# A two-dimensional FFT and a SwiGLU block on one core: rising rows of x in larger blocks, and a build-time planner that knows of DMA transfers

## The chip, the core and the metric

The kernel runs on one core of one Trainium2 chip. The core has five engines, each with its own instruction stream: TensorE (PE) multiplies matrices into PSUM, VectorE (DVE), ScalarE (ACT) and GpSimd (POOL) work elementwise, and SyncE (SP) here only issues DMA transfers. Sixteen DMA engines move the data. The metric is the device time of one execution in microseconds (us).

## The reference

```python
X = np.fft.fft(x, axis=1)          # x: (8, 3008, 256), float32
X = np.fft.fft(X, axis=2)
x = X.real.reshape(8 * 3008, 256)
g = x @ w_gate                     # (256, 1536)
silu = g * (1.0 / (1.0 + np.exp(-g)))
val = x @ w_val                    # (256, 1536)
out = silu * val @ w_out           # (1536, 256) -> (24064, 256)
```

So: the real part of a Fourier transform over sequence and feature, then a gated feed-forward block over 24064 rows.

## The kernel before, in words

**Tables instead of an FFT.** The transforms are matrix products with cosine and sine tables. The symmetries of the input are used first: rows of x and their mirror rows are folded into sums and differences, on the sequence axis (a rising and a falling set of rows) and on the feature axis. The transform over the feature axis is folded into the weights: Wp holds the weights times the cosines, Wq those times the sines, Wm and Wg are signed or scaled copies of Wq. After that each pair of output rows k and M-k comes from the same two vectors P and Q: the row is P W + Q W', its mirror P W - Q W'.

**Loading x.** For each batch b two groups of rows are loaded. XA takes 128 partitions, XC 60 (two batches side by side, one in the upper and one in the lower half). Each partition has eight pieces of 2 KB: four rising (`X3[.., 0:4, :]`), one from each quarter of the sequence, and four falling (`X3[:, 4 + a, :]`), the mirror rows. Rising rows want ascending addresses over the partitions, falling rows descending ones. The kernel therefore cuts the partitions into blocks of L (LA for XA, LC for XC; NA and NC_ are their numbers). The blocks stand in reverse order; within a block, rising rows ascend and falling rows descend. `load_a` (L179) issues NA rising transfers, one a block (L181), and four falling ones over all partitions (L183), whose pattern on the side of x is "NA blocks, then LA rows going down" (`down_set`, L173). `load_c` (L185) does the same for XC: L190 rising, L192 falling, L194 one extra row. In the kernel before LA, NA = 8, 16 and LC, NC_ = 4, 15 (L164, L165).

Batch 0 is loaded at the start by hand (L291 to L314): one rising transfer over all 128 partitions for XA (L291) and two of 64 for XC (L297), and falling rows in the same `down_set` pattern (`fall_a`, L294; `fall_c`, L301), some from SP's queue and some from ACT's. Its rising rows are put into the block order by a matrix product with the permutations putA and putC (`place`, L469); DVE then adds and subtracts (L478 for XA, L572 for XC), and the first transform follows.

**Folding and transforming later batches.** GpSimd folds each load in twelve steps (`fold_steps`, L200; the first of each half is L207, which waits for the load). SP moves the folded XC into a stack of two halves (St, L1285). PE multiplies by the tables (L1299), ACT copies one half (od, L1310) and DVE adds and subtracts into P and Q (L1324).

**The main loop.** The columns are cut into 24 tiles of 328 to 512, and each tile has 12 units (128 of the 1536 hidden columns each). A unit makes gate and value products (PE, L1003), takes them through SiLU (ACT, L1084 and L1115), and multiplies them (DVE L1107 and L1131, or POOL L1103 after an ACT copy, L1100; POOL L1144 for the mirrored half) into hp and hm. KINDS (L32) says for each unit of each tile how the row 0 terms get in and which engine does which part: three groups of twelve letters for gate, value and product. Where KINDS asks for it, the first row of Q, copied to all partitions, is added on DVE (L1069) or seeded into PSUM by ACT (L1059). That copy, bc, is made by two DMA transfers, Q to br (L1444) and br to bc (L1452), for each tile. When a tile is done, its output products (PE, L1171) are evicted by ACT (L1177, L1180) into one of eleven work slots (wk0s to wk10s) and stored by SP in pieces (L1183). The slots also hold the intermediate values of units.

**The planner.** From L806 on the order of all this is set at build time. Each piece is an Op with an engine, a duration, a delay until its result may be used (`lat`), its inputs and outputs. `Sched.run` goes through time, picks for each engine the earliest ready piece within a window, hands out slots and banks, and at the end issues everything in that order. SHIFT holds due times by kind of piece, WINDOW how far ahead an engine may reach. DMA transfers are pieces on SP; the planner also keeps eight `lanes`, since no more than eight transfers may be outstanding: the next one waits until the one eight before it has ended. `run_loads` (L1230) adds up to LOADS load transfers in each unit, and all that are left when the fold begins.

Of the kernel before, what the change touches and what calls it, by code (L numbers as in the profile page):

```python
# [36 lines left out]
    "000000020000 121121122112 DDPDDDDDDDDD",  # L37
    "020202000200 222111121112 DDDDDDPDDDDD",
    "000202020020 121112111211 DDPDDDDDDDDD",
    "002000002222 121211211211 DDDDPDDDDPDD",  # L40
    "020200000000 111211212122 DDDPDDDDDDDD",
    "002020020020 121211112111 PDDDDDDDDDDD",
    "020200000220 111222111112 DDPPDDDDDDDP",
    "002022000220 111122111111 DDPDPDDDDDDD",
    "000002002020 211212121211 PPDDDDDPDDDD",
    "020200000022 111211221112 DDPDDDDDDDPD",
    "020000000222 111112112121 PDDDDDPDDPDP",
    "000200000000 112211222111 DDPPDDDDPDDD",
    "200200202000 121111221211 DPPDPDDDPDDD",
    "220000200020 121211111111 DPDDDDPDDDDD",  # L50
    "002200200022 122111111111 DPDDPDDPPDDD",
    "202002020000 122111111111 DDPPPPPDDPDD",
    "020002220000 211211111111 DPDDDPDPDDDD",
    "002202000200 112211211121 DDDDPDPDDDDD",
    "220220000020 111111111121 PDDPDDPPPDPD",
    "020002220022 111112112211 DPDDPPDPDPDD",
]
# [7 lines left out]
def kernel(  # L65
# [8 lines left out]
    nc = tc.nc  # L74
    B, M, D = x.shape
    Dff = moe_w_gate.shape[1]
    P = 128
# [21 lines left out]
    NCR = GH - P  # L99
# [63 lines left out]

    LA, NA = 8, P // 8  # L164
    LC, NC_ = 4, NCR // 4  # L165

# [619 lines left out]
    for i in range(NS_FIRST, NS):  # L786
# [3 lines left out]
    LOAD_AT = 2  # L790
    LANE = 3.0
    LOAD_LAT = 10.0
    LOADS = 4
    GRP = 4
    WM_ACT = ((1, 0), (1, 1))
    SHIFT = dict(eg=-31.963, egc=-0.628, es=8.915, esc=0.39, ev=-0.141, fold=10.859, gm=5.523, hm=-1.136, hp=6.081,
                 hq=-3.52, od=-3.013, oth=4.215, out=-2.764, pe=-5.12, put=0.935, seedg=1.589, seedv=2.165,
                 sm=2.381, sp=0.129, val=-3.706, vm=5.929)
    WINDOW = {"DMA": 4.725, "PE": 13.96, "ACT": 10.324, "DVE": 14.0, "POOL": 14.0, "SP": 4.726}
    SEM = {"PE": 0.052, "ACT": 0.036, "DVE": 0.036, "POOL": 0.10, "SP": 0.06, "DMA": 0.0}  # L800
    TAIL = {"PE": 0.163, "ACT": 0.118, "DVE": 0.08, "POOL": 0.02, "SP": 0.0, "DMA": 0.0}
    BEGIN = {"DVE": 1.2, "ACT": 0.7, "POOL": 14.0, "PE": 0.0}
    FIFO = {"h": 2, "bc": 2, "br": 1, "pq": 5, "cp": 2, "fc": 1, "st": 3}
    ANY = {"B": 8, "S": NS, "Q": NQ}

    class Op:  # L806
        __slots__ = ("eng", "dur", "lat", "fn", "cat", "clock", "at", "n", "deps", "owners", "new", "start", "free", "end")

    class Sched:
# [11 lines left out]

        def add(self, eng, dur, fn, r=(), w=(), new=(), lat=None, cat="oth", bits=None, after=()):
            o = Op()
            o.eng, o.dur, o.fn, o.n = eng, dur, fn, len(self.ops)
# [24 lines left out]
            o.owners.update(o.new)  # L849
            self.ops.append(o)  # L850

        def run(self, begin, early):
# [25 lines left out]
            order = []  # L878
            lanes = [0.0] * 8

# [43 lines left out]
            while left:  # L924
# [26 lines left out]
                s, o = best  # L951
# [197 lines left out]
    class OWork:  # L1149
# [88 lines left out]
    def fold_step(what, i, unit):  # L1238
# [5 lines left out]
        def fn():  # L1244
            if j == 0:
# [11 lines left out]
        tmp = ("fold",)  # L1257
        r = {0: [((kind,), k) for k in range(40)], 1: [(tmp, "F")], 2: [(tmp, "F")], 3: [(tmp, "E"), (tmp, "O")],
             4: [(tmp, "A")], 5: [(tmp, "E"), (tmp, "O")]}[j]
# [21 lines left out]
    def spread_op(b):  # L1281
        for half, b_ in ((0, b), (1, b + 1)) if b > 1 else ((1, b),):
            for kind in range(2):
                def fn(half=half, b_=b_, kind=kind):
                    nc.sync.dma_start(out=stack(b_)[64 * kind:64 * kind + 64, :],  # L1285
                                      in_=foldC[b][64 * half:64 * half + 64, kind])
                S.add("SP", 0.6, fn, r=[(("fc", b), (q, k)) for q in range(2) for k in range(2)],
                      w=[(("st", b_), kind)], new=[("st", b_)], lat=3.0)

# [169 lines left out]
    S.hold("st", 0)  # L1459
    for fc, at in ((1, 0.0), (2, 6.0)):  # L1460
        for gv in range(2):
            S.add("DMA", 0.01, lambda: None, w=[(("W",), (fc, gv))], lat=at)
    S.add("DMA", 0.01, lambda: None, w=[(("pq", 0), "Q")], lat=0.8)
    S.add("DMA", 0.01, lambda: None, w=[(("Wo",), 0)], lat=9.0)
    prev = None
    owork = None
    U = [Unit(u) for u in units]
    for i, u in enumerate(units):
# [18 lines left out]
        for j, k in enumerate((i - ROW_GAP, i)[::-1]):  # L1487
            tr, fr = divmod(k, nF)
            if k >= 0 and fr == {0: 11, 1: 3, 2: 99}.get(tr, 6) and tr + 1 < nT:
                if j:  # L1490
                    S.add("SP", 0.55, all_rows(tr + 1), r=[(("br", tr + 1), 0)], w=[(("bc", tr + 1), 0)], new=[("bc", tr + 1)], lat=3.0)
                else:
                    S.add("SP", 0.55, first_rows16(tr + 1), r=[(("pq", tr + 1), "Q")], w=[(("br", tr + 1), 0)], new=[("br", tr + 1)], lat=2.6)
        if i == FIRST + 1:
# [59 lines left out]
```

## Time and profile before

| What | Value |
| --- | --- |
| Median of 3 runs | 634.14 us (631.53 to 634.88) |
| The profiled execution | 631.46 us |
| Its span, first to last instruction | 629.7 us |
| Mean granted TensorE clock | 0.995 |
| HBM read and written | 29.43 MB and 24.65 MB |

The profile was taken on the profiled execution alone. A busy row gives an engine's busy time and its share of the span. A row of waits says who waited, what ended the wait, the total, the count and the longest. A row of windows gives a stretch, then for each engine shown its busy time and instructions, then the granted clock, the mean busy share of the 16 DMA engines and GB/s. A chain is the work that ended last, followed back in time. Rows with "SPq" or "ACTq" are the issuing of transfers, not the transfers.

### The profile page before, as it was taken

The page shows a single profiled execution, that of the slowest core. Times are in us where ns is not written, and L with a number is a line of the kernel's source. Part 1 is how long each engine was busy: PE and PEld are TensorE (multiplying, and loading weights), DVE is VectorE, ACT ScalarE, POOL GpSimd, SP SyncE. Part 2 cuts the span into 40 slices and gives each one's busy share as a digit, 9 for nine tenths or more (in the row PEclk, how much of TensorE's full clock was granted, in tenths as well). Part 3 has the DMA queues.
Part 4 walks back from the last instruction along what each step waited for, and adds up shares of the span by engine and source line. Part 5 has one row for each costly group of instructions (what it writes and reads, how often), then busy time and mean ns, then how long its engine had stood idle before and what let it go on. Part 6 is the DMA issues. An engine that isn't in the chain of part 4 may idle for free.

```text
span 629.7 us, 12646 instructions
## 1 busy us (share of the span) xinstructions
PE 607.7 (97%) x4069; PEld 395.8 (63%) x4069; DVE 559.1 (89%) x1030; ACT 572.3 (91%) x1111; POOL 537.1 (85%) x495
## 2 busy tenths in 40 slices
PE   8999998999999899999999999998999999999997
PEld 6545664666556566666666666665666666666686
DVE  8989996988979799899998999877899999999982
ACT  7686667999989799999999999997999999999994
POOL 8878997999789889999999899998899867756782
PEclk9999998999999899999999999999999999999999
DMA  9954447242632712446136112227111112112112
GB/s 227 138 111 119 118 106 165 90 137 74 138 92 59 158 50 88 131 118 151 53 81 155 52 47 59 83 60 165 47 44 52 54 43 61 59 35 61 55 53 77
DMA packets 50736, 57.71 MB, mean 92 GB/s; under 512 B 7256, under 2 KB 37724, under 8 KB 50670
## 3 DMA queue, kind: packets, MB, share of 16 engines
q1 hardware_dynamic: 47016, 53.78, 32.8%
q0 software_dynamic: 3216, 2.36, 2.8%
q10 hardware_dynamic: 438, 0.77, 0.5%
q8 instruction: 32, 0.52, 0.4%
q14 instruction: 34, 0.28, 0.1%
HBM read 29.43 MB, written 24.65 MB: 86 GB/s over the span
## 4 chain that ended last, share of the span: by engine, by line
PE 62%; DMA 16%; POOL 8%; ACT 5%; issue 3%; SPq 3%; DVE 2%; ACTq 0%; POOLq 0%; DVEq 0%
PE ps L1003 31%; PE ps L1171 27%; DMA XA<-in_x_dram 7%; POOL hm L1144 3%; PE ps L1299 3%; DMA XA<-in_moe_w_val_dram 2%; DMA out_dram<-wk5s 1%; POOL SDf L207 1%; DMA br<-Qt 1%; DMA XC<-in_x_dram 1%; ACT ps L1059 1%; SPq L1183 1%; DMA out_dram<-wk1s 1%; DMA out_dram<-wk8s 1%; SPq L181 1%
## 5 line engine op out<-in xcount | busy, mean ns | idle before, releaser
L1003 PE MATMUL ps<-Pt,Wp 128*128 128x512 bf16 (+2 forms) x576 | 206.1, 376 | 8.5 <-ACT wk1s L1310 2.8
L1171 PE MATMUL ps<-Wo,hp 128*128 128x256 bf16 (+2 forms) x1140 | 167.5, 273 | 0.1
L1171 PE MATMUL ps<-Wo,hm 128*128 128x256 bf16 (+2 forms) x1140 | 166.5, 272 | 0.4 <-ACT wk0s L1177 0.3
L1003 PE MATMUL ps<-Qt,Wq 128*128 128x512 bf16 (+2 forms) x422 | 155.2, 377 | 1.9 <-DVE wk1s L1069 1.2
L1171 PEld LDWEIGHTS <-hm 128*128 128x128 bf16 (+2 forms) x1140 | 111.9, 98 | 63.4 <-issue 5.4
L1171 PEld LDWEIGHTS <-hp 128*128 128x128 bf16 (+2 forms) x1140 | 112.0, 98 | 62.7 <-issue 5.9
L1144 POOL TENSOR_TENSOR hm<-sv1q 128x1024 bf16<-128x1024 f32 (+2 forms) x68 | 126.6, 1862 | 25.5 <-ACT sv1q L1115 22.9
L1144 POOL TENSOR_TENSOR hm<-sv0q 128x1024 bf16<-128x1024 f32 (+2 forms) x68 | 126.6, 1862 | 20.8 <-ACT sv0q L1115 17.4
L1059 ACT ACTIVATE ps<-bc,w 128x512 f32<-128x512 bf16 (+2 forms) x154 | 112.4, 738 | 1.2 <-DVE hp L1107 0.3
L1003 PE MATMUL ps<-Qt,Wm 128*128 128x512 bf16 (+2 forms) x294 | 105.2, 376 | 2.6 <-ACT wk5s L1084 2.5
L1003 PEld LDWEIGHTS <-Wp 128*128 128x128 bf16 x576 | 56.5, 98 | 34.5 <-issue 7.1
L1115 ACT ACTIVATE sv0q<-ps 128x512 f32<-128x512 f32 (+2 forms) x101 | 68.8, 686 | 3.5 <-PE ps L1003 2.0
L1115 ACT ACTIVATE sv1q<-ps 128x512 f32<-128x512 f32 (+2 forms) x89 | 61.4, 697 | 3.7 <-PE ps L1003 3.6
L1003 PEld LDWEIGHTS <-Wq 128*128 128x128 bf16 x422 | 41.4, 98 | 28.0 <-issue 9.2
L1003 PEld LDWEIGHTS <-Wm 128*128 128x128 bf16 x294 | 28.8, 98 | 15.1 <-issue 3.8
L207 POOL TENSOR_TENSOR SDf<-XA 128x1020 f32<-128x1020 f32 x14 | 33.0, 2356 | 0.5 <-DMA XC<-in_x_dram 0.3
L1003 PE MATMUL ps<-Qt,Wg 128*128 128x512 bf16 (+2 forms) x82 | 30.5, 372 | 1.3 <-ACT wk2s L1066 1.3
L217 POOL TENSOR_TENSOR Af<-EOf 128x516 f32<-128x516 f32 (+1 forms) x22 | 24.2, 1101 | 0.6
L211 POOL TENSOR_TENSOR EOf<-SDf 128x512 f32<-128x512 f32 (+1 forms) x22 | 24.3, 1105 | 0.0
L214 POOL TENSOR_TENSOR EOf<-SDf 128x512 f32<-128x512 f32 (+1 forms) x22 | 24.1, 1097 | 0.0
L207 POOL TENSOR_TENSOR SDf<-XC 128x1020 f32<-128x1020 f32 (+1 forms) x8 | 18.8, 2351 | 4.3 <-DMA XA<-in_x_dram 4.3
L1069 DVE SCALAR_TENSOR_TENSOR wk2s<-bc,w,ps 128x512 f32<-128x512 bf16 (+1 forms) x30 | 22.3, 742 | 0.0
(435 smaller groups left out, 1398.3 us busy)
## 6 DMA issues: line engine op xcount, KB each, us to landing
XA<-in_x_dram SPq DMA_DIRECT2D x30, 256.0 KB
XA<-in_x_dram SPq DMA_DIRECT2D x112, 64.0 KB
XC<-in_x_dram SPq DMA_DIRECT2D x30, 120.0 KB
XC<-in_x_dram SPq DMA_DIRECT2D x105, 32.0 KB
bc<-br SPq DMA_DIRECT2D x21, 128.0 KB
St<-Fc SPq DMA_DIRECT2D x14, 128.5 KB
out_dram<-wk9s SPq DMA_DIRECT2D x11, 128.0 KB
out_dram<-wk0s SPq DMA_DIRECT2D x11, 128.0 KB
```

The lines of the kernel that those rows point to most:

```text
L181: return ([lambda h=h: q.dma_start(out=X3[LA * h:LA * (h + 1), 0:4, :], in_=up_block(b, JA - LA * h, LA)) for h in range(NA)] + [lambda a= ...
L207: tt(F[:, :, 1:D], up[:, :, 1:D], down[:, :, D - 1:0:-1], op=Alu.add)
L211: tt(E[:, :, 0:P], F[:, :, P:0:-1], F[:, :, P:D], op=Alu.add)
L214: tt(O[:, :, 0:P], F[:, :, P:0:-1], F[:, :, P:D], op=Alu.subtract)
L217: tt(Af[r], EOf[r, :, 0:2, :], EOf[r, :, 2:4, :], op=Alu.add)
L1003: nc.tensor.matmul(ps[:, :n], Wt[:, gv, fs], src[:, :n], start=start, stop=stop, skip_group_check=True)
L1059: nc.scalar.activation(bank(k)[:, :self.wp], bc[self.t][:, :self.wp], AF.Copy, scale=w0[:, gv, self.f:self.f + 1])
L1069: nc.vector.scalar_tensor_tensor(work(e)[:, :self.wp], bc[self.t][:, :self.wp], w0[:, gv, self.f:self.f + 1], bank(k)[:, :self.wp], op0=Al ...
L1115: return lambda: nc.scalar.activation(self.silu(self.sm, w), src()[:, :w], AF.Silu)
L1144: lambda: nc.gpsimd.tensor_tensor(tiles_of(t)[1][:, f - 1:f + 1, :w], pair(self.vm)[:, :, :w, 1], pair(self.vm)[:, :, :w, 0], op=Alu.mult),
L1171: nc.tensor.matmul(bank(ko)[:n, j * D:(j + 1) * D], hts[t][minus][:, f, c:c + n], Wo[:, f, :], start=(f == 0), stop=(f == nF - 1))
L1299: nc.tensor.matmul(ps[:, cols], l, r_, start=(i == 0), stop=(i == len(mms) - 1), skip_group_check=True)
```

## The change

The block sizes go from 8 to 32 partitions (XA) and from 4 to 30 (XC). The rising rows of one batch are then 4 transfers (XA) and 2 (XC) in place of 16 and 15; the falling rows stay at 4 transfers each, with another pattern on the side of x.

The planner gets a line for DMA transfers (`ring`): each transfer on SP has a time for which it holds this line, and ends no earlier than 0.6 us after it; `lanes` now holds those ends. LOAD_LAT, the latencies of stores and of br, bc and St are smaller. Two loads a unit are added in place of four. The rising rows of XA for batch 1 are added at unit 8 as before and the falling ones at unit 12. The weights' arrivals are set later and apart. SHIFT, WINDOW and 22 of the 24 rows of KINDS are replaced.

```diff
@@ KINDS (2 of the 22 new rows)
-    "000000000000 111111111111 DDDDDDDDDDDD",
-    "022200000220 122211112111 DDDDDDDDPPDD",
...
+    "000000000000 111111111111 DDDDDDDPDDDD",
+    "002200020202 211221111221 DDPDDDDDDDDD",
...
-    LA, NA = 8, P // 8
-    LC, NC_ = 4, NCR // 4
+    LA, NA = 32, P // 32
+    LC, NC_ = 30, NCR // 30
...
-    LANE = 3.0
-    LOAD_LAT = 10.0
-    LOADS = 4
+    RING = {"A": 4.0, "C": 2.0}
+    LOAD_LAT = 3.0
+    LOADS = 2
...
-            lanes = [0.0] * 8
+            lanes = [-9.0] * 8
+            ring = 0.0
...
                 if o.eng == "SP":
-                    lanes = lanes[1:] + [o.free + LANE]
+                    ring = max(ring, s + 1.2) + o.ring
+                    o.end = max(o.end, ring + 0.6)
+                    lanes = lanes[1:] + [o.end]
...
-                        S.add("SP", 0.45, lambda ke=ke, args=args: self.store(ke, *args), r=[ke], lat=2.6)
+                        S.add("SP", 0.38, lambda ke=ke, args=args: self.store(ke, *args), r=[ke], lat=2.0, ring=0.002 * args[2] + 0.08)
...
     def run_loads(n):
         for what, k, fn in loads[:n]:
-            S.add("SP", (0.33 if k < 16 else 0.62) if what[0] == "A" else (0.33 if k % 20 < 15 else 0.9), fn,
-                  w=[((what[0],), k)], after=[(("A",), "pre" if k > 15 else "preW")] if what == ("A", 1) else (), lat=LOAD_LAT)
+            up = NA if what[0] == "A" else NC_
+            k_ = k if what[0] == "A" else k % (NC_ + 5)
+            S.add("SP", 0.4 if k_ < up else 0.62 if what[0] == "A" else 0.9, fn, w=[((what[0],), k)], lat=LOAD_LAT,
+                  ring=RING[what[0]] / up if k_ < up else 0.15 if k_ == NC_ + 4 and what[0] == "C" else 0.7 if what[0] == "A" else 0.35,
+                  after=[(("A",), "pre" if k >= NA else "preW")] if what == ("A", 1) else ())
...
-    for fc, at in ((1, 0.0), (2, 6.0)):
-        for gv in range(2):
-            S.add("DMA", 0.01, lambda: None, w=[(("W",), (fc, gv))], lat=at)
+    for fc, gv, at in ((1, 0, 0.5), (1, 1, 3.5), (2, 0, 6.0), (2, 1, 8.5)):
+        S.add("DMA", 0.01, lambda: None, w=[(("W",), (fc, gv))], lat=at)
...
-    S.add("DMA", 0.01, lambda: None, w=[(("Wo",), 0)], lat=9.0)
+    S.add("DMA", 0.01, lambda: None, w=[(("Wo",), 0)], lat=18.0)
...
-        if i == 8:
-            loads[0:0] = ((("A", 1), k, fn) for k, fn in enumerate(load_a(1, nc.sync)))
+        if i in (8, 12):
+            loads[0:0] = [(("A", 1), k, fn) for k, fn in enumerate(load_a(1, nc.sync)) if (k >= NA) == (i == 12)]
...
-                    S.add("SP", 0.55, all_rows(tr + 1), r=[(("br", tr + 1), 0)], w=[(("bc", tr + 1), 0)], new=[("bc", tr + 1)], lat=3.0)
+                    S.add("SP", 0.55, all_rows(tr + 1), r=[(("br", tr + 1), 0)], w=[(("bc", tr + 1), 0)], new=[("bc", tr + 1)], lat=2.5, ring=0.4)
```

The patterns of the loads in the built programs (step and count from the outermost on; SBUF side, then the side of x, in elements):

| Transfer | Before | After |
| --- | --- | --- |
| XA rising, L181 | [4096,8] [512,4] [1,512]; [512,8] [192512,4] [1,512] | [4096,32] ...; [512,32] ... |
| XA falling, L183, L294 | [4096,128] [1,512]; [4096,16] [-512,8] [1,512] | [4096,128] [1,512]; [16384,4] [-512,32] [1,512] |
| XC rising, L190 | [4096,4] [512,4] [1,512]; [512,4] [192512,4] [1,512] | [4096,30] ...; [512,30] ... |
| XC falling, L192 | [4096,60] [1,512]; [2048,15] [-512,4] [1,512] | [4096,60] [1,512]; [15360,2] [-512,30] [1,512] |

In the order of instructions PE has two matmuls fewer, ACT 9 full-width copies more, POOL 10 full-width products more and DVE 10 fewer. SP issues 28 + 14 rising transfers in place of 112 + 105; the lines from L820 on move down by up to seven.

More of the change, by code (lines that the diff above doesn't have):

```diff
@@ L34 @@
     "000000000000 001111001111 DDDDDDDDDDDD",
-    "000000000000 111111111111 DDDDDDDDDDDD",
-    "022200000220 122211112111 DDDDDDDDPPDD",
[L37 to L56, printed above, removed]
+    "000000000000 111111111111 DDDDDDDPDDDD",
+    "002200020202 211221111221 DDPDDDDDDDDD",
+    "000000002000 112111222211 DDDDPPDDDDDD",
+    "200202000000 111222111221 DDDDDDPDPPDD",
+    "202002002200 111111212111 DDDPPDDPDDDD",
+    "000020202000 211212211221 DDDDDDDDDDDD",
+    "200022000202 111111111212 PDPDDDDDDDDD",
+    "002200002000 211121112111 PDDDDPPPDDDD",
+    "220200200020 211112211121 DDPDDDPPDDDD",
+    "002000222002 121111111111 PDDPDPDDDPDD",
+    "000202002200 122112111121 DDDDDDDPDDDD",
+    "202000000220 122121211111 PDDDDDDPPDDD",
+    "002000000020 121111121121 DPDDDDDPPDDD",
+    "220200200020 211111221121 DPPDDPDDDDDD",
+    "002202200000 211111111111 DDPDPPDDPDDD",
+    "002000220200 221111212211 PDDDDDDPDDDD",
+    "200220020200 111121111111 DPDPPDPDDPDD",
+    "002020200022 112122111112 DDDDPDPDPDDD",
+    "000202002000 111121211111 DPDPDDDDDPDP",
+    "200220000000 212111122111 DDPPDPPDPDDD",
+    "000200020200 212111211111 PPDDDPPDPPDD",
+    "000222202220 212111211111 DDDDDDPPDDDD",
 ]
@@ L790 @@
     LOAD_AT = 2
-    LANE = 3.0
-    LOAD_LAT = 10.0
-    LOADS = 4
+    RING = {"A": 4.0, "C": 2.0}
+    LOAD_LAT = 3.0
+    LOADS = 2
     GRP = 4
     WM_ACT = ((1, 0), (1, 1))
[L796 to L800, printed above, removed]
+    SHIFT = dict(eg=-16.927, egc=-6.504, es=16.614, esc=1.135, ev=-1.281, fold=6.925, gm=2.722, hm=0.74, hp=9.149,
+                 hq=3.366, od=-1.036, oth=6.518, out=-2.709, pe=-3.325, put=7.023, seedg=2.388, seedv=1.801,
+                 sm=2.857, sp=0.942, val=1.523, vm=10.422)
+    WINDOW = {"DMA": 7.81, "PE": 7.144, "ACT": 11.872, "DVE": 14.0, "POOL": 12.767, "SP": 6.581}
+    SEM = {"PE": 0.052, "ACT": 0.036, "DVE": 0.036, "POOL": 0.10, "SP": 0.15, "DMA": 0.0}
     TAIL = {"PE": 0.163, "ACT": 0.118, "DVE": 0.08, "POOL": 0.02, "SP": 0.0, "DMA": 0.0}
-    BEGIN = {"DVE": 1.2, "ACT": 0.7, "POOL": 14.0, "PE": 0.0}
+    BEGIN = {"DVE": 1.2, "ACT": 0.7, "POOL": 14.0, "PE": 0.0, "SP": -4.0}
     FIFO = {"h": 2, "bc": 2, "br": 1, "pq": 5, "cp": 2, "fc": 1, "st": 3}
@@ L806 @@
     class Op:
-        __slots__ = ("eng", "dur", "lat", "fn", "cat", "clock", "at", "n", "deps", "owners", "new", "start", "free", "end")
+        __slots__ = ("eng", "dur", "lat", "fn", "cat", "clock", "at", "n", "deps", "owners", "new", "start", "free", "end", "ring")
     class Sched:
@@ L820, in hold, with add @@
             self.live[owner[0]].append(owner)
-        def add(self, eng, dur, fn, r=(), w=(), new=(), lat=None, cat="oth", bits=None, after=()):
+        def add(self, eng, dur, fn, r=(), w=(), new=(), lat=None, cat="oth", bits=None, after=(), ring=0.0):
             o = Op()
+            o.ring = ring
             o.eng, o.dur, o.fn, o.n = eng, dur, fn, len(self.ops)
@@ L1257, in fold_step @@
         tmp = ("fold",)
-        r = {0: [((kind,), k) for k in range(40)], 1: [(tmp, "F")], 2: [(tmp, "F")], 3: [(tmp, "E"), (tmp, "O")],
+        r = {0: [((kind,), k) for k in range(2 * (NC_ + 5))], 1: [(tmp, "F")], 2: [(tmp, "F")], 3: [(tmp, "E"), (tmp, "O")],
              4: [(tmp, "A")], 5: [(tmp, "E"), (tmp, "O")]}[j]
@@ L1287, in spread_op @@
                 S.add("SP", 0.6, fn, r=[(("fc", b), (q, k)) for q in range(2) for k in range(2)],
-                      w=[(("st", b_), kind)], new=[("st", b_)], lat=3.0)
+                      w=[(("st", b_), kind)], new=[("st", b_)], lat=3.0, ring=0.4)
     def transform_op(b, part, eo):
@@ L1490 @@
                 if j:
[L1491 removed]
+                    S.add("SP", 0.55, all_rows(tr + 1), r=[(("br", tr + 1), 0)], w=[(("bc", tr + 1), 0)], new=[("bc", tr + 1)], lat=2.5, ring=0.4)
                 else:
[L1493 removed]
+                    S.add("SP", 0.55, first_rows16(tr + 1), r=[(("pq", tr + 1), "Q")], w=[(("br", tr + 1), 0)], new=[("br", tr + 1)], lat=2.4, ring=0.2)
         if i == FIRST + 1:
```

## The prediction

> **What bounds the kernel now.** I read the page first, then the waits, the chain of waits around the longest ones, then the DMA rows by window.
>
> ```profile
> span 629.7 us, 12646 instructions
> PE 607.7 (97%) x4069; PEld 395.8 (63%) x4069; DVE 559.1 (89%) x1030; ACT 572.3 (91%) x1111; POOL 537.1 (85%) x495
> ```
>
> TensorE (PE) is busy 97%, with ScalarE (ACT) close behind, so the change can win only what PE now waits, some 20 us. Who ends those waits (columns: us in total, times, longest):
>
> ```profile
> PE ps L1003 <- ACT wk1s L1310: 2.8, 1, 2.8
> PE ps L1003 <- ACT wk3s L1126: 2.7, 1, 2.7
> PE ps L1003 <- ACT wk5s L1084: 2.5, 1, 2.5
> PE ps L1003 <- ACT wk2s L1066: 1.3, 1, 1.3
> PE ps L1003 <- DVE wk1s L1069: 1.2, 1, 1.2
> PE ps L1003 <- ACT wk9s L1126: 1.0, 1, 1.0
> ...
> PE ps L1353 <- DMA XA<-in_moe_w_val_dram: 0.9, 1, 0.9
> ```
> ```profile
> ACT wk1s L1310 <- DMA out_dram<-wk1s: 5.0, 1, 5.0
> ACT wk5s L1084 <- DMA out_dram<-wk5s: 3.1, 1, 3.1
> ACT wk3s L1126 <- DMA out_dram<-wk3s: 2.7, 1, 2.7
> ```
>
> PE waits for ACT, and ACT for a store of an output block out of the slot (wk) that it wants to write. The chain at one such place says why the store is late (start, us, what):
>
> ```profile
> 199.64 3.00 DMA XA<-in_x_dram
> 202.66 7.08 DMA XA<-in_x_dram
> 209.76 5.61 DMA XA<-in_x_dram
> 215.38 5.09 DMA out_dram<-wk8s
> ```
>
> The store stands behind loads of x on one queue: the rising rows (L181, L190) and the falling rows (L183, L192). How fast these move is in windows in which almost only one kind is under way (last two columns: mean busy share of the 16 DMA engines, GB/s):
>
> ```profile
> 2.00:6.00 4.00, 4.00 (x40) 4.00 (x39) 3.69 (x24) 1.57 (x5) 3.19 (x6) 1.00 0.91 329
> 114.20:119.00 4.80, 4.80 (x33) 3.11 (x32) 4.73 (x10) 4.76 (x11) 4.80 (x4) 1.00 0.24 69
> 156.60:164.00 7.40, 7.30 (x51) 4.67 (x49) 7.40 (x13) 7.37 (x15) 7.32 (x7) 1.00 0.52 90
> 437.00:440.00 3.00, 1.80 (x14) 1.08 (x12) 0.98 (x2) 1.11 (x3) 1.51 (x2) 1.00 1.02 277
> ```
>
> The second row is rising rows of XC, 4 partitions a transfer: a quarter of the engines. The third is rising rows of XA, 8 partitions: half of them. The fourth is falling rows of XA with stores: all. The first is the start, whole 128-partition transfers: all but 9%. Up to eight transfers are outstanding each time, and yet the share stays at 4/16 and 8/16, so successive small transfers use the same engines. The share follows the count of the outermost step of the transfer's pattern: 4, 8, and for the falling rows of XA 128 on the SBUF side and 16 on the side of x (16 blocks of 8).
>
> **The change, part by part.**
>
> *Rising rows.* Blocks of 32 (XA) and 30 (XC) partitions: 4 transfers for 16 and 2 for 15. The outermost step has 32 and 30 on both sides, so 16 and 15 engines. One batch's rising rows of XA are 1 MiB, at 90 GB/s 11.7 us, at 277 GB/s 3.8 us. Those of XC are 480 KiB: at 69 GB/s 7.1 us, at 15/16 of 277 GB/s 1.9 us. That is 13 us of queue time saved per batch in the slow rows. SP's issue falls too:
>
> ```profile
> L181 SPq DMA_DIRECT2D XA<-in_x_dram x112: 272/293/648, 36.8 to 432.6; - x112
> L183 SPq DMA_DIRECT2D XA<-in_x_dram x28: 536/594/636, 47.1 to 435.1; - x28
> L190 SPq DMA_DIRECT2D XC<-in_x_dram x105: 250/300/2245, 17.4 to 261.0; - x105
> ```
>
> 112 x 0.293 + 105 x 0.300 = 64 us of issuing becomes 42 transfers at some 0.3 to 0.6 us (between the medians of L181 and L183), 13 to 25 us. SP has idle time, so I count this at nothing; what it moves is when transfers start.
>
> *Falling rows.* The same two constants shape these, and nothing else in the diff touches them. The pattern on the side of x becomes 4 blocks of 32 rows for XA (was 16 of 8) and 2 blocks of 30 for XC (was 15 of 4); the SBUF side keeps 128 and 60. No transfer of this trace has a small outermost step on one side only, so the trace leaves open which side counts. From below: the partitions count, and nothing changes. From above: the smaller side counts, and 256 KiB go over 4 engines and 120 KiB over 2. I take the second, because a share can be handed to an engine only if both patterns fall into that many equal outer parts, and in every row above the share is no larger than the smaller side allows. The Trainium skill says it outright ("DMA: Bandwidth & Descriptors", section "Why a DMA increments its semaphore by 16 and not by 1"): the number of engines is the largest up to 16 that divides the slowest dimension of both patterns, and they are the lowest-numbered ones. By that rule 4 and 2 engines, the sum below; the rows for 4, 8 and 16 agree with it, and no run here shows the unequal case yet.
>
> One engine moves 277/16 = 17.3 GB/s (fourth row) to 329/(0.91 x 16) = 22.6 GB/s (first row). Four falling transfers of XA put 256 KiB on each of 4 engines: 11.6 to 15.2 us, against 3.8 at 277 GB/s now. Four of XC put 240 KiB on each of 2: 10.9 to 14.2 us, against 1.9 now.
>
> *The start.* Batch 0 uses falling rows too:
>
> ```profile
> 1.24 1.42 SPq L294 DMA_DIRECT2D XA<-in_x_dram  x2
> 7.56 1.94 SPq L301 DMA_DIRECT2D XC<-in_x_dram  x2
> 3.20 2.34 ACTq L301 DMA_DIRECT2D XC<-in_x_dram  x2
> 13.32 0.67 PE L469 MATMUL ps<-XC,putC 128*128 128x512 f32 x1 [1.01 <-DMA XC<-in_x_dram]
> 14.46 0.42 DVE L572 TENSOR_TENSOR SBc<-ps,XC 128x256 bf16<-128x256 f32 x1 [0.89 <-PE ps L469]
> ```
>
> PE at 13.32 waits for the last rising rows of XC; VectorE (DVE) at 14.46 needs the falling rows of XC, and the first tile of the main loop needs what it writes. So these loads are on the path with hardly any cover. The two busiest engines would carry 64 KiB of the first transfer, 256 of falling XA, 32 of rising XC and 240 of falling XC: 592 KiB against 190 now. At 17.3 to 22.6 GB/s that is 35 to 27 us from about 2 us on, so L572 starts at 29 to 37 instead of 14.46: +15 to +23. I take 20 GB/s: **+18**.
>
> *The first row copy.* The falling rows of batch 1 are issued just ahead of br, in both kernels:
>
> ```profile
> 49.76 4.51 DMA br<-Qt
> 54.29 2.34 DMA bc<-br
> 56.68 2.15 DMA br<-Qt
> ```
>
> With nothing ahead br takes 2.15, behind the tail of four falling transfers 4.51; bc waits for br, and PE for bc (the 1.2 us row of L1069 above). Four transfers of 11.6 to 15.2 us in place of 3.8 move br by 8 to 11 us, and there is no cover: **+8**.
>
> *The later loads.* Per batch XA takes 10 to 16 us of queue now (1 MiB at the 90 GB/s of the third row, or at 8 x 22.6 = 181 at best, is 11.7 to 5.8, plus 3.8), XC 9. It becomes 15 to 19 and 13 to 16. Queued behind: SP stands still while bc waits for br, with the stores after it; ACT waits for their slots, PE for ACT. POOL in L207 waits for x, with hm behind it, which the output products need. So stores, br and bc stay behind loads as long as now or longer, and the engines 0 to 3 that carry the falling rows are in every full-width store. What 6 more loads of XA and 3 pairs of XC cost beyond today's waits lies between -15 (all six rows of L1003 above gone, 11.5, plus 3.2 of clock, below) and +45 (5 us for each of 9). Lateness of several us costs today 2.5 to 2.8 where it costs at all, so I take **+12**.
>
> *The planner.* It now believes 0.7 and 0.35 us a falling transfer and 3 us of latency, so it sets stores and row copies nearer to loads than they will be served. That is inside the +12. The weights' later arrival moves the last of the four weight products back by some five matmuls; the 0.9 us of L1353 above goes, by that or behind the late start: -1. The new KINDS leave PE two matmuls fewer (-0.4); ACT makes 9 more full-width copies and DVE 10 fewer products, at 0.6 to 0.7 us each, which matters only if PE is fed:
>
> ```profile
> 300.00:350.00 50.00, 50.00 (x335) 32.56 (x334) 47.15 (x79) 49.97 (x99) 47.86 (x43) 1.00 0.37 94
> 90.00:100.00 10.00, 7.20 (x51) 4.67 (x49) 6.59 (x20) 4.44 (x8) 9.92 (x12) 0.93 0.57 109
> 100.00:150.00 50.00, 49.74 (x328) 32.37 (x327) 43.89 (x76) 48.79 (x97) 45.12 (x43) 0.98 0.48 132
> 200.00:250.00 50.00, 47.16 (x308) 30.57 (x307) 44.78 (x83) 45.00 (x87) 44.08 (x39) 0.97 0.42 95
> ```
>
> In the first of these rows ACT is full beside PE. The others show a granted clock of 0.93, 0.98 and 0.97 around and behind the 2.8 and 2.5 us waits: 0.7 + 1.0 + 1.5 = 3.2 us. The Trainium skill ("TensorE: Matmul & The Clock Gate", section "Part 1: The HAM clock gate") has the clock halved after an idle window of about 3.4 us, until as long a busy one. By that the long wait at the start would add about 1.7 us, not in my sum; the trace agrees in kind, though its dips come after slightly shorter waits.
>
> *Sum.* 631.46 (the profiled execution; its span is 629.7) + 18 + 8 + 12 - 1.4 = 668. The median of the three runs is 634.14, 0.4% above the profiled one, so a median of the changed kernel would be at about 671. I say **670**.
>
> **The rivals.**
>
> *Falling rows keep their engines* (the partitions count). Then queue time per batch falls from 19 to 25 us to 11.4 (3.8 + 3.8 + 1.9 + 1.9), the stores come in time and PE loses its six waits (11.5 us) and the 3.2 of clock: 631.5 - 14.7 = 617. With ACT full, its copies may give 5 back: 617 to 622. For it: the trace has no unequal pattern below 16, so nothing in it excludes this. Against it: no row shows a share above the smaller side's count. Chance 0.13.
>
> *Few engines, slower by the start alone.* The rising rows hand back in the steady part what the falling rows take, and even today's waits go: 631.5 + 15 + 8 - 15 = 640. For it: stores late by several us often cost nothing today. Chance 0.24.
>
> *Few engines, and the row copies stall too.* In four places the new order has br or bc between falling rows of one load; each could wait 5 to 10 us, with POOL held at L207 for x. With the dear end of the start: 631.5 + 23 + 11 + 45 = 710. Chance 0.15.
>
> *Within 0.5%* (about what a measurement of this kernel can tell from no change), if the start is hidden by something that I take for critical: 0.03. The forecast itself, 650 to 690: 0.45.
>
> **How the numbers follow.** The three cases with few engines hold 0.84 and reach from 636 to 714; the faster case and the draw are left out with 0.16. Slower 0.84, same 0.03, faster 0.13.
>
> **What would show it.** Windows of falling rows alone have a DMA share of 0.25 (XA) and 0.13 (XC) instead of 1.0, and rising rows near 1.0. L572 starts at 29 to 37 us, and PE has an idle stretch of over 10 us before it, ended by a DMA into XC. The first br takes 10 us or more to land. The waits for stores behind XA remain. If falling rows show a share near 1.0 and L572 starts near 14, my step on the engines is wrong and the time is near 618.

## The result, and the profile after

| | Before | After |
| --- | --- | --- |
| Median of 4 runs each, on one chip | 632.84 us (631.21 to 634.88) | 704.12 us (702.53 to 705.56) |
| Ratio, after to before | | 1.112, 95% interval 1.108 to 1.117 |
| The profiled execution, its span | 631.46, 629.7 us | 703.92, 702.1 us |
| Mean granted TensorE clock | 0.995 | 0.943 |

The changed kernel is 11% slower: 71.3 us more on the median and 72.4 us more of span, where the sum of the prediction was 36.6. The time lies inside the range (636 to 714), and outside the forecast itself (650 to 690). The page of the changed kernel, to be held against the two rows of before:

```profile
span 702.1 us, 12487 instructions
...
PE 623.1 (89%) x4005; PEld 401.9 (57%) x4067; DVE 559.3 (80%) x1027; ACT 575.9 (82%) x1119; POOL 547.1 (78%) x501
```

ACT and DVE do nearly what they did before (+3.6 and +0.2 us), POOL 10.0 us more, in a longer span: they wait. PE's busy time grew by 15.4 us with two matmuls fewer (and 62 of the 4067 are missing from this trace), so some of them ran slower.

**How many engines a falling row touches.** Windows of the changed kernel; the last two columns are the mean busy share of the 16 DMA engines and GB/s, PEclk stands ahead of them:

```profile
158.00:163.00 5.00, 0.64 (x4) 0.20 (x2) 0.01 (x1) 0.00 (x0) 3.45 (x4) 0.83 0.13 46
...
206.00:208.00 2.00, 0.00 (x0) 0.00 (x0) 0.00 (x0) 0.00 (x0) 0.00 (x0) 1.00 0.26 99
...
210.00:212.00 2.00, 1.21 (x5) 0.69 (x5) 1.81 (x3) 2.00 (x5) 0.83 (x2) 0.50 0.00 0
...
242.00:244.00 2.00, 2.00 (x17) 1.51 (x16) 2.00 (x6) 2.00 (x5) 2.00 (x3) 1.00 1.03 224
```

The first row has falling rows of XC in flight: 0.13 is 2 engines of 16. The second has falling rows of XA: 0.26 is 4. The fourth is mostly rising rows of XA: all 16. In the second row all five engines stand still for 2 us while four DMA engines work off what is queued. The third row is 2 us later: the matmuls are back at 210.79, behind a PE wait of 6.50 us, at half the granted clock.

**The start.** DVE and PE of the changed kernel (start, us, what, then in brackets the idle time ahead of it and what ended it):

```profile
29.00 0.76 DVE L572 TENSOR_TENSOR SBc<-ps,XC 128x256 bf16<-128x256 f32 x2 [7.63 <-DMA XC<-in_x_dram]
35.26 1.09 DVE L572 TENSOR_TENSOR SBc<-ps,XC 128x256 bf16<-128x256 f32 x3 [5.51 <-DMA XC<-in_x_dram]
```
```profile
15.19 1.44 PE L523 MATMUL ps<-Tab,EOb 128*128 128x377 bf16 x4 [4.13 <-ACT EOb L536]
21.91 3.38 PE L469 MATMUL ps<-XC,putC 128*128 128x512 f32 x4 [5.28 <-DMA XC<-in_x_dram]
25.13 0.81 PE L523 MATMUL ps<-Tab,EOb 128*128 128x377 bf16 x4
29.48 0.83 PE L530 MATMUL ps<-Tab,SBc 128*128 128x377 bf16 x2 [3.55 <-DVE SBc L572]
35.75 2.09 PE L530 MATMUL ps<-Tab,SBc 128*128 128x378 bf16 x6 [5.44 <-DVE SBc L572]
...
43.20 0.37 PE L1007 MATMUL ps<-Pt,Wp 128*128 128x480 bf16 x1
```

L572 waits twice for falling rows of XC and starts at 29.00 (before: 14.46). The same four matmuls at L523 take 1.44 us in the first row and 0.81 in the third: that is the half clock. The main loop (L1007) begins at 43.20, before at 22.22.

**The main loop.** Of the waits between 60 and 620 us, the six longest that name a DMA (total, times, longest):

```profile
DVE wk2s L1073 <- DMA bc<-br: 11.2, 1, 11.2
ACT wk0s L1130 <- DMA out_dram<-wk0s: 8.3, 2, 6.6
DVE wk4s L1073 <- DMA out_dram<-wk4s: 7.6, 1, 7.6
ACT wk5s L1119 <- DMA out_dram<-wk5s: 6.9, 1, 6.9
ACT wk6s L1088 <- DMA out_dram<-wk6s: 5.9, 1, 5.9
ACT ps L1063 <- DMA bc<-br: 5.7, 1, 5.7
...
```

The kinds of wait are those of before, stores and row copies, but longer and more of them. The first of them in the chain:

```profile
151.01 11.79 DMA br<-Qt
162.80 0.02 issue
162.81 0.02 SPq L1459
162.83 0.03 issue
162.86 5.81 DMA bc<-br
```

SP's queue around that place shows what they stand behind (an x4 row is four transfers):

```profile
144.76 2.73 SPq L192 DMA_DIRECT2D XC<-in_x_dram  x4
...
150.24 0.67 SPq L192 DMA_DIRECT2D XC<-in_x_dram  x1
151.01 2.82 SPq L1451 DMA_DIRECT2D br<-Qt  x1
...
158.47 1.33 SPq L192 DMA_DIRECT2D XC<-in_x_dram  x2
162.86 0.60 SPq L1459 DMA_DIRECT2D bc<-br  x1
```

Where the 72.4 us arise, by the start of each tile's first product in the two traces (after minus before): +21.0 at tile 0, +19.4 at tile 1, +27.1 at tile 2, +44.0 at tile 5, +61.0 at tile 9, +70.2 at tile 13, and +72.4 at the end. So the start, and then steps of 5 to 13 us as long as batches are loaded. The first of these steps, 7.7 us from tile 1 to tile 2, is a store's: three pieces of wk5s are issued from 79.23 us on, between falling rows of XC, ACT waits 6.9 us for the slot (L1119), and PE behind it:

```profile
87.03 0.59 PE L1007 MATMUL ps<-Pt,Wp 128*128 128x512 bf16 x1 [5.74 <-ACT wk5s L1119]
```

### The profile page after: what moved, and what is told of

Read it like the earlier page. It is cut to its first block, busy times and chain, and to the rows that moved or that the text cites. A ratio compares the mean times of both kernels' runs of the same rounds, so it can differ in the third digit from the quotient of the medians.

```text
span 702.1 us, 12487 instructions
## 1 busy us (share of the span) xinstructions
PE 623.1 (89%) x4005; PEld 401.9 (57%) x4067; DVE 559.3 (80%) x1027; ACT 575.9 (82%) x1119; POOL 547.1 (78%) x501
## 4 chain that ended last, share of the span: by engine, by line
PE 54%; ACT 20%; DMA 18%; issue 3%; DVE 2%; SPq 1%; ACTq 1%; DVEq 0%
PE ps L1007 28%; PE ps L1175 23%; DMA XC<-in_x_dram 4%; ACT ps L1063 3%; DMA br<-Qt 3%; ACT sv1q L1119 3%; DMA out_dram<-wk1s 3%; DMA out_dram<-wk0s 2%; DMA out_dram<-wk2s 2%; PE ps L1306 2%; ACT sv0q L1119 2%; DMA bc<-br 2%; DMA out_dram<-wk4s 1%; SPq L1187 1%; DMA out_dram<-wk5s 1%
## 5 line engine op out<-in xcount | busy, mean ns | idle before, releaser
L1007 PE MATMUL ps<-Pt,Wp 128*128 128x512 bf16 (+2 forms) x562 | 209.9, 384 | 33.8 <-ACT ps L1063 12.1
L1175 PE MATMUL ps<-Wo,hp 128*128 128x256 bf16 (+2 forms) x1140 | 172.5, 279 | 7.7 <-DVE hp L1111 6.8
L1175 PE MATMUL ps<-Wo,hm 128*128 128x256 bf16 (+2 forms) x1140 | 170.5, 276 | 0.3
L1175 PEld LDWEIGHTS <-hp 128*128 128x128 bf16 (+2 forms) x1140 | 114.4, 101 | 83.3 <-issue 19.2
L1007 PE MATMUL ps<-Qt,Wq 128*128 128x512 bf16 (+2 forms) x386 | 145.9, 385 | 4.0 <-DVE wk2s L1073 3.5
L1063 ACT ACTIVATE ps<-bc,w 128x512 f32<-128x512 bf16 (+2 forms) x155 | 117.4, 768 | 6.5 <-DMA bc<-br 5.7
L1007 PE MATMUL ps<-Qt,Wm 128*128 128x512 bf16 (+2 forms) x281 | 107.1, 387 | 9.1 <-ACT wk2s L1088 4.9
L1007 PEld LDWEIGHTS <-Wp 128*128 128x128 bf16 x576 | 57.2, 99 | 32.3 <-issue 10.2
L1119 ACT ACTIVATE sv0q<-ps 128x512 f32<-128x512 f32 (+2 forms) x96 | 69.1, 723 | 0.9 <-PE ps L1007 0.9
L1119 ACT ACTIVATE sv1q<-ps 128x512 f32<-128x512 f32 (+2 forms) x92 | 64.7, 709 | 0.3 <-PE ps L1007 0.3
L1007 PEld LDWEIGHTS <-Wq 128*128 128x128 bf16 x421 | 41.9, 100 | 22.2 <-issue 8.5
L1007 PEld LDWEIGHTS <-Wm 128*128 128x128 bf16 x291 | 29.0, 100 | 31.1 <-issue 14.6
L1007 PE MATMUL ps<-Qt,Wg 128*128 128x512 bf16 (+2 forms) x82 | 31.5, 384 | 0.4 <-ACT wk10s L1070 0.2
L1073 DVE SCALAR_TENSOR_TENSOR wk2s<-bc,w,ps 128x512 f32<-128x512 bf16 (+2 forms) x20 | 14.5, 723 | 11.2 <-DMA bc<-br 11.2
L1111 DVE TENSOR_TENSOR hp<-wk0s,ps 128x512 bf16<-128x512 f32 (+2 forms) x23 | 15.4, 670 | 9.1 <-ACT wk0s L1130 8.1
```

The lines of the kernel that those rows point to most:

```text
L1007: nc.tensor.matmul(ps[:, :n], Wt[:, gv, fs], src[:, :n], start=start, stop=stop, skip_group_check=True)
L1063: nc.scalar.activation(bank(k)[:, :self.wp], bc[self.t][:, :self.wp], AF.Copy, scale=w0[:, gv, self.f:self.f + 1])
L1073: nc.vector.scalar_tensor_tensor(work(e)[:, :self.wp], bc[self.t][:, :self.wp], w0[:, gv, self.f:self.f + 1], bank(k)[:, :self.wp], op0=Al ...
L1111: lambda: nc.vector.tensor_tensor(tiles_of(t)[0][:, f, :wp], work(self.sp)[:, :wp], bank(v)[:, :wp], op=Alu.mult),
L1119: return lambda: nc.scalar.activation(self.silu(self.sm, w), src()[:, :w], AF.Silu)
L1175: nc.tensor.matmul(bank(ko)[:n, j * D:(j + 1) * D], hts[t][minus][:, f, c:c + n], Wo[:, f, :], start=(f == 0), stop=(f == nF - 1))
```

## The experiments

The theory is that of the prediction: falling rows on 4 and 2 engines cost the time, in the start and behind the loads of the loop. Rivals: the new schedule loses it, or any larger rising block does. Every run has its own runs of the kernel before on the same chip, so the ratios compare across tables. Spans compare less well: the chips' medians of the kernel before lie between 626.09 and 632.84 us.

### The parts of the change, apart

`e1_old_blocks`, the changed kernel with the old sizes:

```diff
-    LA, NA = 32, P // 32
-    LC, NC_ = 30, NCR // 30
+    LA, NA = 8, P // 8
+    LC, NC_ = 4, NCR // 4
```

> The changed kernel (its schedule, its planner's times) with the blocks of before: LA 8, LC 4, so falling rows have outermost steps 16 and 15 again and rising rows 8 and 4. Theory (the falling rows on 4 and 2 engines cost the 72 us): the start is that of before (first tile of the main loop at about 22 us), falling rows of XA land about 0.9 us apart instead of 2.55, and the time is near that of before, 625 to 645 us; the planner now takes 0.25 us of queue for a rising row transfer, so some late stores remain. Rival (the new schedule itself loses the time, since it packs stores and row copies closer to the loads): the start comes back, some 21 us, but the time stays at 670 to 685 us.

`e2_old_plan`, the kernel before with the new sizes (the same lines the other way, and the tests for "is a rising row" in `run_loads` made to follow them):

> The kernel of before (its schedule, its planner's times) with the new blocks 32 and 30, nothing else of the change. Theory: the loss comes with the blocks: start +21 us, the later loads +40 to +55 us, half clock for tens of us, time 690 to 710 us. Rival (the new schedule loses the time): only the start is lost, 645 to 660 us.

`e3_xa_alone`: `LA, NA = 32, P // 32` with `LC, NC_ = 4, NCR // 4`.

> The changed kernel with blocks of 32 for XA alone; XC is back at 4 (rising on 4 engines, falling on 15). Theory: falling rows of XA still land 2.55 us apart, those of XC under 1 us apart. Start: without the 2-engine rows PE starts the main loop later than before by the XA rows alone, +5 to +12 us; later loads: 7 of the 10 slow loads are XA's, so 30 to 45 of the 51 us stay. Time 665 to 690 us. Rival (the order of the schedule, not the transfers): as e1_old_blocks within 10 us.

`e4_xc_alone`: `LA, NA = 8, P // 8` with `LC, NC_ = 30, NCR // 30`, and the fold again waits for every piece of a load (`range(40)`, as before), since XA has more pieces than XC here.

> The changed kernel with blocks of 30 for XC alone; XA is back at 8 (rising on 8 engines, falling on 16). Theory: the XC rows hold the start: +12 to +20 us there; later only the XC loads (three pairs and one single) stall, 10 to 20 us. Time 650 to 670 us. If the two losses add, e3_xa_alone and e4_xc_alone over e1_old_blocks together give about 72 us. Rival (the start is set by XA's falling rows): start under +8 us and the time within 15 us of e1_old_blocks.

| Kernel | Median us | Ratio to before (95%) | First tile at, us | Span |
| --- | --- | --- | --- | --- |
| e1_old_blocks | 627.86 | 1.000 (0.997 to 1.004) | 22.3 | 626.4 |
| e2_old_plan | 712.01 | 1.135 (1.126 to 1.143) | 44.3 | 711.6 |
| e3_xa_alone | 672.31 | 1.071 (1.064 to 1.078) | 33.6 | 671.0 |
| e4_xc_alone | 665.06 | 1.062 (1.055 to 1.070) | 37.1 | 663.5 |

The block sizes bring the loss: without them the new schedule is as fast as the old, and with them the old one is even slower (2 us over what I expected). The rest of the change, with two constants that its description leaves out (0.15 us until SP sees another engine's end, in place of 0.06, and SP's begin at -4.0 us), is in e1_old_blocks. XA's part (44.6 us of span over e1_old_blocks) and XC's (37.1) add to 81.7, a little more than both together (75.7); I had expected about 72. In e4_xc_alone 22.3 of the 37.1 come after the start, a little over the 10 to 20 that I expected. At the start the wait of XC is the larger (14.8 us later than e1_old_blocks) and XA's 11.3 lies partly under it. e2_old_plan has all its matmul records, so it splits the loss:

```profile
span 711.6 us, 12462 instructions
...
PE 632.1 (89%) x4069; PEld 405.4 (57%) x4069; DVE 560.1 (79%) x1030; ACT 575.5 (81%) x1111; POOL 539.4 (76%) x495
```

Against before, with the same 4069 matmuls, PE is busy 24.4 us longer (the matmuls at half clock) and stands idle 57.5 us longer (711.6 - 632.1 against 629.7 - 607.7). On average, a us of waiting thus cost 0.4 us more behind it.

### Other transfers for the falling rows

`e5_pool_queue` and `e6_pool_start`:

```diff
-[lambda a=a: q.dma_start(out=X3[:, 4 + a, :], ...
+[lambda a=a: nc.gpsimd.dma_start(out=X3[:, 4 + a, :], ...
...
+            if up <= k_ < up + 4:
+                S.add("POOL", 0.75, fn, w=[((what[0],), k)], lat=8.0, ...
```

The diff shows the line of XA and the planner's; the line of XC (`load_c`) is changed the same way. In e6_pool_start `fall_a` and `fall_c` of the start go to POOL as well.

> The changed kernel with the falling rows of the main loop issued by POOL on its own queue instead of by SP; the start is left as it is. In the changed kernel's trace POOL's loads into 2 partitions and into 128 partitions all touch 16 engines. Theory (the count of engines, set by the smaller outermost step, and the queue that br, bc and stores share with the falling rows): in the main loop both the wait behind the falling rows and the narrow transfers go, so only the start stays, +21 us and some clock: 645 to 662 us, POOL some 25 us busier. Rival (falling rows steal engine time wherever they are issued, their 4 and 2 engines stay): stores and row copies still pass the same engines and PE still idles over 45 us: 680 to 705 us. Rival (POOL becomes the bound by issuing): 670 us or more with POOL over 95% busy.

> As e5_pool_queue, and the falling rows of the start are issued by POOL too. Theory: 16 engines for these as well, so the first tile of the main loop begins at 22 to 28 us instead of 43, and the time is that of before or a little less, 615 to 640 us. Rival (the start is lost to the number of bytes or to issuing, not to the count of engines): the start stays over 35 us and the time equals that of e5_pool_queue.

`e7_middle_blocks`: `LA, NA = 16, P // 16` and `LC, NC_ = 10, NCR // 10`.

> The changed kernel with blocks of 16 (XA) and 10 (XC): rising rows on 16 and 10 engines, falling on 8 and 6. By the theory the queue time of a batch goes as 1/rising + 1/falling engines: XA 1/16 + 1/8 as before (1/8 + 1/16), XC 1/10 + 1/6 = 0.27 against 1/4 + 1/15 = 0.32 before and 1/30 or 1/15 + 1/2 = 0.57 after. So the later loads cost nothing against before, and the start, where only falling rows are narrower, loses 2 to 6 us: 628 to 640 us. Rival (any larger rising block costs, in proportion to its growth): about a third of the way to the changed kernel, 645 to 665 us.

| Kernel | Median us | Ratio to before (95%) | First tile at, us | Span |
| --- | --- | --- | --- | --- |
| e5_pool_queue | 676.40 | 1.080 (1.076 to 1.083) | 43.9 | 673.4 |
| e6_pool_start | 663.57 | 1.060 (1.054 to 1.066) | 28.3 | 661.9 |
| e7_middle_blocks | 631.78 | 1.007 (1.004 to 1.010) | 29.5 | 630.8 |

The time of e7_middle_blocks came out as reckoned: falling rows on 8 and 6 engines cost 7.2 us at the start (1 more than I allowed) and nothing later (+4.5 at the end). So it isn't the size of the rising blocks. For XA, what rising rows gain in engines falling rows lose, since LA times NA is 128; the sum of the two times is as small at 16 and 8 as at 8 and 16.

e5_pool_queue and e6_pool_start both missed. The start of e6_pool_start went as expected (+6.0 at the first tile over e1_old_blocks, where e5_pool_queue keeps +21.6), and the first four falling rows of XC in e5_pool_queue's loop landed 0.4 to 0.6 us apart (from 67.5 us on), not 2.4 to 3.5; the later ones are issued further apart and land so. But the loops still lost 25 and 30 us. A stretch in which e5_pool_queue lost some 15 of them:

```profile
88.00:125.00 37.00, 26.59 (x151) 15.46 (x150) 22.53 (x35) 14.72 (x27) 36.45 (x45) 0.91 0.45 108
```
```profile
101.20 1.91 POOL L1148 TENSOR_TENSOR hm<-sv0q 128x1024 bf16<-128x1024 f32 x1
103.05 0.65 POOL L220 TENSOR_TENSOR CEa<-Af 128x258 bf16<-128x258 f32 x1
103.65 0.64 POOL L221 TENSOR_TENSOR CEa<-Af 128x258 bf16<-128x258 f32 x1
104.23 0.69 POOL L192 DMA_DIRECT2D XC<-in_x_dram  x1
```

POOL, the fifth busy time, works 36.45 of 37 us, with folds and issues of 0.7 us ahead of the products hm that the slots and PE wait for. e1_old_blocks has POOL as full between the same two tiles (26.84 of the 27 us from 72 to 99), without the issues. Over the whole span of e5_pool_queue it is 87% busy, so "over 95%" as the sign of a POOL bound was the wrong question: it is the bound in the stretches where it folds and loads. This is read from the trace; no run tests it.

### What the planner believes

Left open: the prediction put the planner's belief inside its term for later loads. `e8_true_times` leaves every transfer as it is and corrects the belief:

```diff
-... else 0.7 if what[0] == "A" else 0.35,
+... else 2.6 if what[0] == "A" else 3.0,
```

> The changed kernel, its planner told 2.6 and 3.0 us of queue for a falling row of XA and XC (what its trace shows) instead of 0.7 and 0.35; transfers are the same. Theory (the transfers themselves are too long for the queue): the order adapts, some stores are moved, but the start stays and most of the loop's loss too: 680 to 704 us. Rival (the loop's loss is the planner's wrong belief): only the start is lost, 645 to 665 us.

It gave 648.96 us, ratio 1.036 (1.033 to 1.039). **My theory fell and the rival stood.** First tile at 43.2 as in the changed kernel (+20.9 over e1_old_blocks), +20.8 us at the end: on balance, all that is left over e1_old_blocks is the start. Waits for DMA in its loop, same window as above, all of them:

```profile
DVE wk2s L1073 <- DMA bc<-br: 11.7, 1, 11.7
POOL hm L1148 <- DMA XA<-in_x_dram: 1.8, 1, 1.8
POOL SDf L207 <- DMA out_dram<-wk6s: 0.4, 1, 0.4
POOL SDf L207 <- DMA out_dram<-wk5s: 0.3, 1, 0.3
ACT wk3s L1130 <- DMA out_dram<-wk3s: 0.3, 1, 0.3
```

The waits for stores are down to 1.0 us in all, with the same narrow transfers on the same queue. The one long wait for bc (near 150 us) cost 10.6 us at tile 5, and the loop had won 8 of them back by tile 17. Are the stores less late, then? SP's queue near 95 us, first in the changed kernel, then in e8_true_times:

```profile
92.55 2.79 SPq L192 DMA_DIRECT2D XC<-in_x_dram  x4
95.39 1.16 SPq L194 DMA_DIRECT2D XC<-in_x_dram  x1
96.64 1.23 SPq L1187 DMA_DIRECT2D out_dram<-wk4s  x3
```
```profile
91.26 3.71 SPq L192 DMA_DIRECT2D XC<-in_x_dram  x3
95.07 1.21 SPq L1187 DMA_DIRECT2D out_dram<-wk6s  x3
```

Both stores stand behind falling rows of XC, and both are late: in the changed kernel they land at 107.2 to 107.7 us, 13.9 us after their block was ready, in e8_true_times at 104.3 to 104.8, 18.3 us after it. In the changed kernel DVE waits 7.6 us for that slot, and PE behind it:

```profile
109.20 1.25 PE L1175 MATMUL ps<-Wo,hp 128*128 128x256 bf16 x5 [6.82 <-DVE hp L1111]
```

In e8_true_times nobody waits for this store; the slot's next writer starts at 109.9 us. So the true times don't make the stores early. The planner reckons with the late end of a store and gives the next block another slot, or other work comes first; which of the two, the trace doesn't tell apart. The late store that was reckoned with cost nothing here, and the one that came later than planned cost PE 6.8 us. That is no rule: the bc near 150 us cost 10.6 us in the plan with true times too.

Is that the belief, or one lucky order? Two more doses (the same line with 1.3 and 1.5, and with 5.2 and 6.0), and the belief of the kernel with old blocks put right (`e9_old_true`):

```diff
 # e9_old_true, over e1_old_blocks
-    RING = {"A": 4.0, "C": 2.0}
+    RING = {"A": 12.0, "C": 6.3}
...
-... else 0.7 if what[0] == "A" else 0.35,
+... else 0.95 if what[0] == "A" else 0.75,
```

> The changed kernel, its planner told 1.3 and 1.5 us of queue for a falling row: half of what e8_true_times was told. Theory (the loop's loss grows with the error of the belief): between the changed kernel and e8_true_times, 660 to 690 us. Rival (e8_true_times was a lucky order, since each order of such a planner differs by tens of us): no order among the doses; as likely over 700 us as under 650 us.

> The changed kernel, its planner told 5.2 and 6.0 us: twice what the trace shows. Theory (what is planned late enough costs nothing, so an error to the slow side is cheap): 645 to 665 us, near e8_true_times. Rival (lucky order): as for e11_half_told, over 680 us as likely as not.

> e1_old_blocks (blocks 8 and 4, the new schedule), its planner told the queue times that this kernel's trace shows: 0.75 and 0.42 us for a rising row transfer of XA and XC instead of 0.25 and 0.13, 0.95 and 0.75 for a falling one instead of 0.7 and 0.35. If a wrong belief about the queue is what costs (theory after e8_true_times), the few waits behind stores go: 618 to 626 us, which would be below both kernels. Rival (with these blocks the believed times were near enough; the rest is fixed): 625 to 631 us, the same as e1_old_blocks.

`e10_true_pool_start` is e8_true_times with the start of e6_pool_start:

> e8_true_times with the falling rows of the start issued by POOL, where they touch 16 engines; the main loop keeps its falling rows on 4 and 2 engines. Theory (the loss is the start plus a plan that believes wrong times, and the two add): the start falls from +21 to about +6 us, as in e6_pool_start, and the time to 630 to 640 us. Rival (with an earlier start the narrow loads of the loop stall again, since the order was right only for the late start): 645 us or more.

| Falling row of XA, XC: time told, us | Kernel | Median us | Ratio to before (95%) | Span |
| --- | --- | --- | --- | --- |
| 0.7, 0.35 | the changed kernel | 704.12 | 1.112 (1.108 to 1.117) | 702.1 |
| 1.3, 1.5 | e11_half_told | 688.53 | 1.098 (1.091 to 1.104) | 685.9 |
| 2.6, 3.0 | e8_true_times | 648.96 | 1.036 (1.033 to 1.039) | 647.2 |
| 5.2, 6.0 | e12_double_told | 666.20 | 1.061 (1.055 to 1.066) | 664.6 |
| 2.6, 3.0 | e10_true_pool_start | 648.01 | 1.032 (1.025 to 1.040) | 646.3 |
| old blocks, 0.95, 0.75 | e9_old_true | 618.19 | 0.985 (0.981 to 0.990) | 615.2 |

The doses stand in order, with the least at what the trace shows. Telling too much costs too (17 us, 1 more than I allowed), against 55 for too little (by the ratios, 0.077 of the kernel before or 48 us). How far orders of this planner scatter at one dose was not tried; each dose is one order, so all of these differences could hold some of that.

e9_old_true is the best of all, 1.5% under the kernel before and 1.5% under e1_old_blocks, by the belief alone (one order here as well):

```profile
span 615.2 us, 12727 instructions
...
PE 603.5 (98%) x4067; PEld 394.5 (64%) x4067; DVE 557.7 (91%) x1027; ACT 572.9 (93%) x1119; POOL 545.5 (89%) x501
```

Against e9_old_true, whose plan has true times too, e8_true_times is not free in the loop: it is 32.0 us longer (647.2 and 615.2), 20.8 at the first tile and 11.2 after it. So narrow falling rows cost something even where the plan knows of them.

e10_true_pool_start missed, and shows why: its main loop begins 12 us earlier than that of the changed kernel (31.4), but by tile 2 it is 19.1 us behind e1_old_blocks, where e8_true_times is 18.5 behind. SP's queue:

```profile
46.88 1.74 SPq L181 DMA_DIRECT2D XA<-in_x_dram  x4
49.75 8.94 SPq L183 DMA_DIRECT2D XA<-in_x_dram  x4
58.78 3.12 SPq L1451 DMA_DIRECT2D br<-Qt  x1
70.71 0.62 SPq L1459 DMA_DIRECT2D bc<-br  x1
```

The first br takes 11.9 us behind four falling rows of XA, and bc lands at 73.1 us, within a us of the changed kernel's 73.9. From the first tile (+9.1) to tile 2 (+19.1) it falls 10 us further back. 3.8 of these arise in tile 0, where PE waits 2.4 us for a weight transfer (L1360); 6.2 arise in tile 1, where DVE waits 2.7 us for bc and PE 2.4 us behind it. The narrow loads of batch 1 set when the first row copy can land; a late start hides that, an early one lays it bare. Here the two costs didn't add.

## Why the prediction was right in sign and short in size

- **The count of engines: right.** 0.26 and 0.13 in the windows for 4 and 2 of 16, as forecast (0.25, 0.13): the smaller outermost step counts, also where the SBUF side has 128 or 60. The Trainium skill's rule ("DMA: Bandwidth & Descriptors", section "Why a DMA increments its semaphore by 16 and not by 1") holds here in the unequal case: by it 4 and 2 engines, by the windows as many.
- **The start, +18: right, +21.0.** L572 began at 29.00, the early end of 29 to 37, and its second part, which the first tile follows, at 35.26. What the sum leaves out is the clock: the matmuls of this stretch ran partly at half of it. My sign for it, one idle stretch of PE of over 10 us, did not come; there are four of 3.6 to 5.4 us, with work between them.
- **The first row copy, +8: next to nothing.** br took 7.11 us and not 10 or more. The copy is wanted in tile 1: there bc landed at 73.9 us, DVE waited 0.8 us for it and PE not at all (before: 1.2 us of PE). The late start covered it. e10_true_pool_start shows the price with less cover: 6.2 us in tile 1. The step that failed is "there is no cover": I added two waits for the same loads.
- **The later loads, +12 within -15 to +45: mis-sized, +51** (72.4 - 21.0), above its own upper bound. Two things in it failed. "It now believes 0.7 and 0.35 us a falling transfer ... That is inside the +12" hid the largest term: with true times and the same transfers the loop costs nothing on balance over e1_old_blocks (e8_true_times), so the 54.9 us between the spans of the changed kernel and e8_true_times go with the belief. And 5 us a stall was too cheap: the steps are 5 to 13 us.
- **The clock: left out of the sum** as 1.7 us. In e2_old_plan it is 24.4 us of longer matmuls, in the changed kernel at least 15.4 (62 records are missing). "TensorE: Matmul & The Clock Gate", section "Part 1: The HAM clock gate", in the Trainium skill, by which the clock is halved after an idle window of about 3.4 us, was read for the one long wait at the start. In the loop the half clock came eight times, behind PE waits of 3.1 to 6.8 us, so it bears on these as well.
- **The rest of the change: right at about nothing.** The new schedule with the old blocks measures 1.000.
- **The rivals.** 704 lies by the case "few engines, and the row copies stall too" (710, chance 0.15). Its picture was right in that row copies and stores stall, and only half right in why: br and the stores stand behind falling rows, which they do in e8_true_times too, and the planner doesn't know for how long. That 704 lies inside the range is owed in part to the range's width: of the three terms, one was right, one measured nothing and one was four times its size.

So, in spans of the profiled executions: 626.4 for the new schedule with the old blocks, plus 20.8 for the start, plus 54.9 that go with the belief, is 702.1 (rounded terms). The 3.3 between 629.7 and 626.4 are no gain of the schedule: on one chip the two kernels take the same time. The belief's part holds for these transfers; with the old blocks a smaller error cost 11.2 us (626.4 and 615.2).

## What to carry to other kernels

A block size that shapes two transfers has two effects: work out the outermost count on both sides for each, for what one gains in engines the other can lose. When a schedule is made at build time, check its durations against the trace of the very transfers it will issue: an error of 2 to 3 us a transfer cost some 50 us here, and putting a smaller one right won 1.5% where the transfers were good. Look at lateness against the plan first, and at lateness itself after it. Waits for one load at two places need not add, and a wait of several us costs more than itself where the matmuls after it run at half clock.

## What was unexpected of the hardware

- Few engines run faster each: 99 GB/s on 4 and 46 on 2 are 25 and 23 GB/s for one, against 17.3 where all 16 move falling rows of XA and stores (277 GB/s). With whole 128-partition loads, at the start of the kernel before, 16 engines reached 22.6 each.
- Waits of only 3.6 to 5.4 us were followed by half clock for about 10 us twice in the start (from 14.5 and from 28.2 us in the changed kernel); in all, its span has 80 us at half clock, that of before 7.
- The same falling rows, issued by POOL, filled the DMA engines, with the patterns that gave 2 and 4 engines from SP's and ACT's queues: from 64 to 66 us of e5_pool_queue, with little else under way, the share was 1.11 at 192 GB/s.
